# Retention and ELU layer on one core: the first block's retention in whole chunks of 128 tokens

## The chip, the cores and the metric

The kernel runs on one core of one Trainium2 chip. The metric is the device time of one execution in microseconds (us), the median of three runs. An engine [...] waits at an instruction until the semaphores that it names have come. The engines are called PE (TensorE, matrix products; its weight loads are listed apart as PEld), DVE (VectorE), ACT (ScalarE), POOL (GpSimd) and SP (SyncE, which here only issues DMAs).

## The reference

Retention with 8 heads of 64 over 4 sequences of 768 tokens, then a layer with an ELU between two weight matrices:

```
gamma[h] = 1 - 2**(-5 - h);  scale = 1/sqrt(64)
for t:  state = gamma * state + k[t] v[t]^T ;   y[t] = scale * q[t] state
x = y as (3072 tokens, 512)
h = x @ w_in            # 512 x 2048
g = h if h > 0 else exp(h) - 1
out = g @ w_out         # 2048 x 512
```

All of it is in 32-bit floats. The powers of gamma are taken out of the recursion: v is scaled by `gamma**-t / 8` (table `vf`), the result by `gamma**t` (table `etab`, seen as `powers`), and between the two the retention is a causal product without decay: the scores q k^T are masked to the past and multiplied with v, and q times the state (the sum of k v^T over all earlier pieces) is added.

## The kernel before, in words

The 3072 tokens go through in six blocks of 512. A block is four chunks of 128 tokens; one DMA brings a chunk (`load`, L110): q and k turned, with two heads above one another in the 128 partitions, and k and v with tokens in the partitions. The weights come in 16 pieces of 1 MB as 64-bit patterns (`load_piece`, L142) and are decoded into floats: two or three ACT steps (`prepare`, L164 to L168), then DVE steps (`decode`, L190 to L194). The step that takes the high words (`hi`) is ACT's L168, or DVE's L190 if `by_vector` is set. Pieces 0, 2, 4 and 6 are the halves `w_a` of the first matrix, pieces 1, 3, 5 and 7 the halves `w_b`.

The order of the work of each engine is written out by hand: instructions stand in each queue in the order in which the program calls for them. Generators (`decode` with `take`, `plain_first` as `inner`, `outputs_of_first`) are drawn on step by step to lay their parts between one another. Two things concern the change.

**Retention of a block (sub-chunks of 64 tokens).** Every product is a tile of 64 rows by 64 columns of the PE array, 64 elements long, so four of them can lie in the array at once. Per chunk there are 16 products of each of four kinds: scores (L307, from `score_products`), the sum k v^T of each half chunk (L338, `state_products`), scores times v (L394, `within`) and q times the state (L409, `across`). There is one state for every 64 tokens (`state`, `state_sum`, L348 or L350). The mask is a 64 by 64 triangle (`cmask`, L328 or L318). [...] the work is cut in two, and a small DVE copy (`seen`, L426 or L378) between the halves makes PE wait for the first half. DVE takes the result out of the PSUM times `powers` (L433 or L384) into `xb`.

In the first block chunk 0 and chunk 1 go one by one (`score_products`, `mask_pair`, `outputs_of_first`), chunks 2 and 3 as a pair (`scores(0, 1)`, `states(0, 1)`, `outputs(0, 1)`). The later blocks use the pair form throughout.

**First matrix on the first block (`plain_first`).** There are 16 tiles of 128 output rows over 512 tokens, four products each. Tiles 0 to 4 are done by halves of 256 tokens, because the second half of the tokens comes late: tile 0 in its first half even by chunks of 128 tokens. Tiles 5 to 15 are done in one go (L521). Tile k is in the PSUM bank "aabd"[k], tile 4 in a bank of the pool `ps_r` (`hp`). Tiles 0 to 3 need pieces 0 and 1, tile 4 needs piece 2. Behind every tile ACT and DVE form the ELU (L477, L478, L481).

At the start PE has nothing to do until the first chunk lands: one blank product of 512 columns and 28 blank products of 64 columns run (L1106, L1110). Three more blank products lie between the first steps (one of 256, two of 512 columns, `unread`).

The table `etab` for tokens 0 to 255 is built by ACT at the start (L249); the rest is built between the two halves of piece 0's `prepare` (argument `between`).

## Time and profile before

| | us |
|---|---|
| three runs | 633.62, 634.01, 636.01 (median 634.01) |
| the profiled execution, its own time | 632.87 |
| its span, first to last instruction | 630.9 |
| PE busy in the span | 624.8 (99%) |
| DVE, ACT, POOL busy | 483.1, 253.3, 21.8 |
| granted clock of TensorE | 1.00 |

The span is 1.97 us shorter than the execution's own time. A page of the profile and further views are used: sums by stretches of time; the timeline, which gives for each group of instructions its start, how long it lasts, engine, line, operation and tile, count, and in brackets how long the engine had been idle before it and what ended that; and the waits, which say who waited for whom. A product of 32-bit floats appears as two records of PE, so that "x8" on a line of PE is four products.

### The profile page before, as it was taken

How to read it: one execution, taken by the hardware profiler on the slowest of the kernel's cores; microseconds unless marked ns; L12 is line 12 of the kernel's file. 1: busy time of each engine (PE TensorE's matmuls, PEld its weight loads, DVE VectorE, ACT ScalarE, POOL GpSimd, SP SyncE). 2: the span in 40 equal slices, each digit the busy share in tenths (PEclk: the TensorE clock that was granted, in tenths of full speed). 3: DMA queues.
4: the chain of work that ended last, by engine and by line, in shares of the span. 5: the costliest groups of instructions: out<-in, count | busy, mean ns of one | idle time of the engine just before them, and what ended most of it. 6: DMA issues, size and time to landing. Idle time of an engine off the chain costs nothing.

```text
span 630.9 us, 16128 instructions
## 1 busy us (share of the span) xinstructions
PE 624.8 (99%) x6680; PEld 560.1 (89%) x6680; DVE 483.1 (77%) x884; ACT 253.3 (40%) x472; POOL 21.8 (3%) x25
## 2 busy tenths in 40 slices
PE   8999999999999999999999999999999999999998
PEld 5864578888899999889999989999988999988997
DVE  5779789989789675699685588777489877558975
ACT  6698635015541114653112646111465211366311
POOL 1021000000000000200000200000110000000000
PEclk9999999999999999999999999999999999999999
DMA  8698669689287888405888702888810798600794
GB/s 331 278 406 291 188 210 268 196 267 316 81 311 248 239 255 299 180 2 174 274 266 292 282 2 64 264 284 296 310 73 12 216 308 252 217 18 2 232 309 162
DMA packets 75897, 136.85 MB, mean 217 GB/s; under 512 B 6320, under 2 KB 31792, under 8 KB 70704
## 3 DMA queue, kind: packets, MB, share of 16 engines
q1 hardware_dynamic: 75824, 135.82, 64.8%
q8 instruction: 53, 0.87, 0.5%
q14 instruction: 20, 0.16, 0.1%
HBM read 114.56 MB, written 21.23 MB: 215 GB/s over the span
## 4 chain that ended last, share of the span: by engine, by line
PE 77%; SPq 1%; DVE 1%; DMA 1%; issue 0%; ACT 0%; ACTq 0%; DVEq 0%
PE pa L955 20%; PE pa L913 10%; PE pd L955 10%; PE pb L955 5%; PE pa L867 5%; PE pb L913 4%; PE pa L740 4%; PE qa L913 3%; PE pd L867 2%; PE qd L913 2%; PE pd L913 2%; PE pd L740 2%; PE y L394 1%; PE sc L307 1%; PE y L409 1%; PE kv L338 1%
## 5 line engine op out<-in xcount | busy, mean ns | idle before, releaser
L963 ACT COPY ms<-pa 128x128 f32<-128x128 f32 x104 | 27.7, 266 | 146.7 <-PE pa L955 146.7
L955 PE MATMUL pa<-ts,wq 128*128 128x128 f32 x560 | 74.2, 275 | 0.0
L955 PE MATMUL pd<-ts,wq 128*128 128x128 f32 x552 | 73.5, 276 | 0.0
L955 PEld LDWEIGHTS pa<-ts,wq 128*128 128x128 f32 x560 | 68.5, 192 | 0.4
L955 PEld LDWEIGHTS pd<-ts,wq 128*128 128x128 f32 x552 | 67.1, 192 | 0.6 <-DVE res L967 0.2
L955 PE MATMUL pa<-gC,wq 128*128 128x128 f32 x480 | 64.7, 278 | 0.0
L478 ACT ACTIVATE r<-r 128x512 f32<-128x512 f32 x96 | 60.5, 630 | 3.1
L955 PEld LDWEIGHTS pa<-gC,wq 128*128 128x128 f32 x480 | 59.0, 192 | 1.5 <-issue 0.3
L477 ACT ACTIVATE r<-gC 128x512 f32<-128x512 f32 x64 | 39.9, 624 | 32.4 <-DVE gC L921 32.4
L967 DVE TENSOR_TENSOR res<-pd,ms 128x128 f32<-128x128 f32 x68 | 19.5, 287 | 39.6 <-PE pd L955 38.4
L481 DVE SCALAR_TENSOR_TENSOR gC<-r,gC 128x512 f32<-128x512 f32 x64 | 44.0, 719 | 0.7 <-ACT r L478 0.7
L829 DVE TENSOR_TENSOR ts<-gC,ts 128x512 f32<-128x512 f32 x60 | 41.3, 688 | 1.0
L829 DVE TENSOR_TENSOR ts<-gC 128x512 f32<-128x512 f32 x60 | 41.0, 684 | 0.0
L281 POOL TENSOR_TENSOR chunk<-chunk,vf 128x512 f32<-128x512 f32 x16 | 20.0, 1251 | 428.8 <-DMA chunk<-in_qkv_dram 345.8
L955 PE MATMUL pb<-gC,wq 128*128 128x128 f32 x240 | 31.7, 275 | 0.0
L988 ACT COPY res<-pa 128x128 f32<-128x128 f32 x34 | 9.0, 266 | 55.0 <-PE pa L955 55.0
L955 PEld LDWEIGHTS pb<-gC,wq 128*128 128x128 f32 x240 | 29.2, 192 | 0.0
L690 ACT COPY m<-pa 128x512 f32<-128x512 f32 x24 | 13.9, 581 | 30.2 <-PE pa L740 16.3
L921 DVE TENSOR_TENSOR gC<-qa,gC 128x512 f32<-128x512 f32 x8 | 5.5, 692 | 25.0 <-PE qa L913 18.3
L913 PE MATMUL pa<-xt,w_b 128*128 128x256 f32 x96 | 23.0, 382 | 0.0
L913 PE MATMUL pa<-xt,w_s 128*128 128x256 f32 x96 | 23.0, 382 | 0.0
L913 PE MATMUL pa<-xb,w_a 128*128 128x256 f32 x96 | 22.7, 379 | 0.0
(255 smaller groups left out, 1244.3 us busy)
## 6 DMA issues: line engine op xcount, KB each, us to landing
wq<-scratch_dram SPq DMA_DIRECT2D x277, 256.0 KB, 4.3
chunk<-in_qkv_dram SPq DMA_DIRECT2D x23, 1024.0 KB, 8.6
wraw<-in_w_dram SPq DMA_DIRECT2D x15, 1024.0 KB, 6.0
out_dram<-res SPq DMA_DIRECT2D x14, 256.0 KB, 3.8
scratch_dram<-gT SPq DMA_DIRECT2D x12, 256.0 KB, 4.3
scratch_dram<-m SPq DMA_DIRECT2D x12, 192.0 KB, 6.0
scratch_dram<-so SPq DMA_DIRECT2D x4, 512.0 KB, 4.6
scratch_dram<-wi SPq DMA_DIRECT2D x2, 1024.0 KB, 6.4
```

Source lines behind the costliest of these rows:

```text
L281: eng.tensor_tensor(out=kv[:, 1], in0=kv[:, 1], in1=vf[:, i].unsqueeze(2).to_broadcast([C, H, D]), op=ALU.mult)
L477: nc.scalar.activation(e, h, AF.Relu, scale=-1.0)
L478: nc.scalar.activation(e, e, AF.Exp, scale=-1.0)
L481: nc.vector.scalar_tensor_tensor(g, e, -1.0, h, ALU.add, ALU.max)
L690: nc.scalar.copy(m, ps)
L740: nc.tensor.matmul(ps[:, fi, :], lhsT=w[:, fi, j2, :], rhs=x[:, j2, :], start=(begin and fi == 0 and j2 == 0), stop=(j2 == 1), skip_group_ ...
L829: sub = lambda o, x, y: nc.vector.tensor_tensor(out=o, in0=x, in1=y, op=ALU.subtract)
L867: nc.tensor.matmul(ps[:, f, :], lhsT=lhs[f], rhs=xs[j][k], start=(begin and f == 0), stop=True, skip_group_check=True,)
L913: nc.tensor.matmul(ps[:, fi, :], lhsT=w[:, fi, j2, :], rhs=x[:, j2, :], start=(j in (1, 7) and fi == 0 and j2 == 0), stop=(j2 == 1), skip_ ...
L955: nc.tensor.matmul(ps, lhsT=w[:, f, :], rhs=ts[j][k][:, f, :], start=(begin and f == 0), stop=(f == 3), skip_group_check=True,)
L963: nc.scalar.copy(m, ps)
L967: nc.vector.tensor_tensor(out=o, in0=x, in1=y, op=ALU.add)
```

## The change

For the first block alone, retention is done in chunks of 128 tokens (`whole_...`). Per chunk there are 8 products of each kind in place of 16:

- scores: 64 rows by 128 columns of the array, 128 long (all of the 128 by 128 scores of a head, also those that the mask sets to zero);
- scores times v: 128 rows by 64 columns, 128 long;
- q times the state: 64 by 64, 128 long, not for chunk 0;
- sum k v^T: 128 rows by 64 columns, 64 long.

There is one state per chunk and one addition per state. The mask is the 128 by 128 triangle `causal`; masked scores go partly over k in the chunk's buffer, partly to a new tile `pt`. The copies `seen` are gone. Chunks 2 and 3 are taken one by one, with tile 2 of the layer between their scores. Tile 4 is done in one go; tile 3 has its first half by chunks of 128 tokens. Blank products: 22 in place of 28 short ones; of the three `unread` one of 512 stays. The rest of `etab` is built after piece 1's `prepare`; the second half of piece 0 has its high words taken by DVE.

```diff
-        for k in range(5):
-            hp = bank("aabd"[k]) if k < 4 else ps_r.tile([P, 2, TH], FP32, name="hp", tag="r")
-            banks.append(hp.rearrange("p a b -> p (a b)"))
-            if k == 0:
-                part(0, slice(0, C))
+        for k in range(4):
+            banks.append(bank("aabd"[k]).rearrange("p a b -> p (a b)"))
+            if k in (0, 3):
+                part(k, slice(0, C))
                 yield
-                part(0, slice(C, 2 * C))
+                part(k, slice(C, 2 * C))
...
+    def whole_scores(m):
+        qk = raw[m][0]
+        sc = [ps_r.tile([P, HP, C], FP32, name="sc", tag="r") for _ in range(2)]
+        for p in range(HP):
+            for a in range(2):
+                nc.tensor.matmul(
+                    sc[a][:, p, :], lhsT=qk[rows(a), 1, p, :], rhs=qk[rows(a), 0, p, :],
+                    start=True, stop=True, skip_group_check=True,
+                )
+        more = hpool.tile([P, TB], FP32, name="pt", tag="h")
+        whole[m] = sc, (qk[:, 1], more.rearrange("p (h c) -> p h c", c=C))
+
+    def whole_mask(m, a):
+        sc, pt = whole[m]
+        nc.vector.tensor_tensor(
+            out=pt[a], in0=sc[a], in1=causal.unsqueeze(1).to_broadcast([P, HP, C]), op=ALU.mult
+        )
+
+    def whole_within(m, y, a):
+        pt, kv = whole[m][1], raw[m][1]
+        for u in range(2):
+            for c in range(2):
+                nc.tensor.matmul(
+                    y[a][rows(c), u, :], lhsT=kv[:, 1, head(a, u, c), :], rhs=pt[a][:, 2 * u + c, :],
+                    start=(u == 0), stop=(m == 0), skip_group_check=True,
+                )
+
+    def whole_across(m, y):
+        q = raw[m][0]
+        for u in range(2):
+            for c in range(2):
+                for a in range(2):
+                    p = 2 * u + c
+                    nc.tensor.matmul(
+                        y[a][rows(c), u, :], lhsT=state(0, 2 * m)[rows(a), p, :], rhs=q[rows(a), 0, p, :],
+                        start=False, stop=True, skip_group_check=True,
+                    )
+
+    def whole_products(m):
+        kv = raw[m][1]
+        t = ps_r.tile([P, HP, D], FP32, name="kv", tag="r")
+        for p in range(HP):
+            for a in range(2):
+                nc.tensor.matmul(
+                    t[rows(a), p, :], lhsT=kv[:, 0, 2 * p + a, :], rhs=kv[:, 1, 2 * p + a, :],
+                    start=True, stop=True, skip_group_check=True,
+                )
+        return t
+
+    def whole_sum(m, t):
+        if m:
+            nc.vector.tensor_tensor(out=state(0, 2 * m + 2), in0=t, in1=state(0, 2 * m), op=ALU.add)
+        else:
+            nc.vector.tensor_copy(state(0, 2), t)
+
+    def whole_end(m, y):
+        c = slice(m * C, (m + 1) * C)
+        for a in range(2):
+            j = slice(2 * a, 2 * a + 2)
+            nc.vector.tensor_tensor(out=xb[:, j, c], in0=y[a], in1=powers[:, j, c], op=ALU.mult)
+
+    def whole_place(m):
+        ts = [bank("bd"[a]) if m < 2 else ps_r.tile([P, 2, TH], FP32, name="y", tag="r") for a in range(2)]
+        return [t.rearrange("p a b -> p (a b)")[:, 0:TH].rearrange("p (u t) -> p u t", u=2) for t in ts]
```

The order of the first block's calls, written out by hand, after the change:

```
unread(1, TB); 22 short blank products
whole_scores(0); whole_mask(0, 0); scale_v(0); whole_mask(0, 1)
y = whole_place(0); whole_within(0, y, 0)
t = whole_products(0); whole_sum(0, t); whole_within(0, y, 1); whole_end(0, y)
unread(1, TB)
whole_scores(1)
prepare(2, by_vector=(False, True)); piece = decode(True); take(); take()
scale_v(1); whole_mask(1, 0); whole_mask(1, 1); take()
inner = plain_first(); next(inner)                    # tile 0, chunk 0
y = whole_place(1); whole_within(1, y, 0); whole_within(1, y, 1); whole_across(1, y)
whole_end(1, y); take()
t = whole_products(1); whole_sum(1, t); take()
prepare(2, by_vector=True); powers_of(slice(2 * C, S))
next(inner)                                           # tile 0 chunk 1, tile 1 first half
piece = decode(); take()
whole_scores(2); next(inner)                          # tile 2 first half
scale_v(2, True); whole_mask(2, 0); whole_mask(2, 1); take()
whole_scores(3); scale_v(3, True)
y = whole_place(2); whole_within(2, y, 0); whole_within(2, y, 1); whole_across(2, y)
t = whole_products(2); whole_mask(3, 0); whole_end(2, y); whole_mask(3, 1); whole_sum(2, t)
take(); prepare(2); next(inner)                       # tile 3, chunk 0
y = whole_place(3); whole_within(3, y, 0); whole_within(3, y, 1); whole_across(3, y)
next(inner); whole_end(3, y)                          # tile 3, chunk 1
piece = decode(True); take(); take()
t = whole_products(3); whole_sum(3, t)
take(); take(); take(); prepare()
```

After it come the second halves of tiles 0 to 3 and the tiles 4 to 15, as before.

## The prediction

> **What bounds the kernel now.** First the sums by stretches, cut where PE's work changes its nature: to 5.15 us (before the first chunk), to 15.92 (chunks 0 and 1), to 38.21 (chunks 2 and 3, tiles 0 to 4), then the rest.

> ```profile
> core 0: us, PE busy (x) PEld busy (x) DVE busy (x) ACT busy (x) POOL busy (x), PEclk, DMA share, GB/s
> 0.00:5.15 5.15, 3.70 (x58) 2.09 (x59) 2.40 (x23) 2.60 (x5) 1.56 (x8) 1.00 0.63 173
> 5.15:15.92 10.77, 9.56 (x258) 6.76 (x255) 6.83 (x19) 7.85 (x14) 0.17 (x1) 1.00 1.02 411
> 15.92:38.21 22.29, 21.96 (x337) 18.68 (x337) 17.03 (x32) 15.39 (x21) 0.46 (x1) 1.00 0.77 307
> 38.21:120.00 81.79, 81.79 (x731) 54.81 (x730) 71.21 (x109) 50.52 (x57) 5.86 (x4) 1.00 0.80 264
> ```

> The first column is the length, the second PE's busy time. From 38.21 PE never stops, and the waits of PE over the whole span are all of the first 28 us; the chain of waits is 77% PE. So whatever the change does must show as the time at which tile 5 (L521) starts, 38.21 before, and it goes one to one to the end. In the second stretch PE is covered by blank products and waits for DVE and DMA. Here is the third:

> ```profile
> 15.92 3.10 PE L497 MATMUL pa<-xb,w_a 128*128 128x128 f32 x16
> 18.93 1.99 PE L497 MATMUL pb<-xb,w_b 128*128 128x256 f32 x8
> 20.86 1.16 PE L307 MATMUL sc<-chunk 64*64 64x64 f32 x64
> 21.84 1.11 PE L338 MATMUL kv<-chunk 64*64 64x64 f32 x64
> 22.88 1.99 PE L497 MATMUL pd<-xb,w_b 128*128 128x256 f32 x8
> 24.81 1.50 PE L394 MATMUL y<-chunk 64*64 64x64 f32 x63
> ...
> 27.09 0.69 PE L409 MATMUL y<-chunk 64*64 64x64 f32 x32 [0.26 <-DVE seen L378]
> 27.78 1.97 PE L497 MATMUL hp<-xb,w_a 128*128 128x256 f32 x8
> ```

> The reader is to see that scores and sums take about 1 us each for two chunks, but L394 and L409 take 27.78 - 24.81 = 2.97 us: about 1.1 us of it are waits for states and for `seen`. That is what can be won, with 0.25 us of wait for piece 1 before 18.93.

> **Prices on PE.** A product is two records. An undisturbed four products of 128 columns take 0.89 us (190.12 to 191.01 below), of 256 columns 1.73 us (38.21 back to 36.49). The next lines are a group of the later blocks, and one of chunk 0:

> ```profile
> 186.11 1.06 PE L955 MATMUL pa<-ts,wq 128*128 128x128 f32 x8
> 187.10 2.10 PE L307 MATMUL sc<-chunk 64*64 64x64 f32 x128
> 189.12 1.16 PE L955 MATMUL pa<-gC,wq 128*128 128x128 f32 x8
> 190.12 1.06 PE L955 MATMUL pb<-gC,wq 128*128 128x128 f32 x8
> 191.01 1.06 PE L955 MATMUL pa<-gC,wq 128*128 128x128 f32 x8
> ```

> ```profile
> 8.42 0.45 PE L409 MATMUL pd<-chunk 64*64 64x64 f32 x8
> ```

> Small products go in steps: L409 at 14.68, 14.73 and 14.79 us starts four records each time, 0.058 us apart. 32 such steps are 1.87 us, L307 takes 2.02 to the next start, L955 before it 0.99 instead of 0.89 and after it 1.00: one excursion to small tiles and back costs 0.35 us beyond the work, 0.13 going in and 0.22 coming out. The one line of L409 is chunk 0's, where only one row half has a state: 8 records in 0.45 us, of which 0.22 is the length of the last. One after another at 0.058 they would need 0.63, so two column halves on the same rows do run side by side.

> [...] the modes 64x128 and 128x64 stand nowhere in the trace of before. [...] the blanks of 64 columns step at 0.107 us, L307 at 5.15 still does, and at 10.66 the step is 0.058.

> **The change on PE, per chunk.** Before: 16 products of a kind are 8 steps, 0.47 us, four kinds 1.87 us. After: scores, two side by side, 128 long: 8 products = 16 records = 8 steps of 0.112 (half of 0.89 by 4), 0.89 us. Scores times v: the same, 0.89. q times state: four side by side, 0.45. Sums: two side by side, 64 long, 0.47. Total 2.70, so 0.83 us more per chunk, because the scores that the mask kills are now computed and multiplied. More modes too: see below.

> **DVE.** 128x256 masks (L328) at 0.38 each become 128x512 at 0.60 to 0.69:

> ```profile
> 7.07 0.75 DVE L328 TENSOR_TENSOR chunk<-sc,cmask 128x256 f32<-128x256 f32 x2
> 22.07 1.29 DVE L318 TENSOR_TENSOR chunk<-sc,cmask 128x512 f32<-128x512 f32 x2 [0.35 <-PE sc L307]
> ```

> Against that fall six `seen` (0.16 to 0.25) and four additions of states (0.42). Per block DVE stays about equal; its order matters more.

> **Chunks 0 and 1, walked.** Landings, from issue and time to landing in the DMA view: chunk 0 at 5.1 (q, k) and 6.4 (k, v), first half of piece 0 at 8.1, chunk 1 at 10.6, second half of piece 0 at 12.6, piece 1 at 15.0, chunk 2 at 17.5, chunk 3 at 20.2. None of these is moved: SP's queue starts the same. The six blank products fewer end 0.3 us sooner (3 of their 14 steps of 0.107) and lie before 5.15, where PE waits for the landing: nothing, with that landing as cover; without it they would give 0.3. The two `unread` that go (0.70 and 0.9 us) lay in waits: nothing either. Scores of chunk 0 start at 5.15, half at the slow clock, ready about 6.65; mask 7.39, v scaled 7.99, PE goes on at 8.04 and is through by 9.4; results in `xb` at 10.3, where before it was 10.05. Piece 0's first half is decoded at 11.35 (11.44 before): equal. Chunk 1's scores start at 10.66, as before, bound by the landing, and end 0.42 later; masks ready at 12.56 and 13.16 (12.71 before). But then nothing waits for `seen`: scores times v to 13.66, q times state to 14.25, results in `xb` at 14.85 and 15.2 (before 15.85), and the sums end at 14.86. Tile 0's second chunk starts at **15.06 instead of 15.92**. Tile 1 needs piece 0's second half: its DVE step (L194) comes behind the results, done at 15.8; tile 1 starts at 16.05. High words by DVE (L190, 0.42) lie ahead of that, at 13.3, in DVE's wait for chunk 1's products.

> **From there to tile 5.** Work in order: tile 0 0.89, tile 1 1.73, scores 0.89, tile 2 1.73, scores 0.89, chunk 2's other products 0.89 + 0.45 + 0.47, tile 3 0.89, chunk 3's 0.89 + 0.45, tile 3 0.89, sums 0.47, second halves of four tiles 6.91, tile 4 in one go 3.45: 21.9 us. Before, the same stretch held 20.2; the difference is twice the 0.83 per chunk. Changes of mode: 4 from the layer into retention (0.13), 4 back (0.22), and 4 between forms of retention, not in the trace: bounds 0 and 0.22, I take 0.15, near the two measured. Sum 2.0 us against 0.7 before (two excursions). Tile 5 then starts at 15.06 + 21.9 + 2.0 = **38.95, 0.7 us later** than 38.21.

> Does something else come later still? Chunk 2 is there at 17.5, PE asks at 17.9; chunk 3 at 20.2, asked at 20.9. DVE by the same walk: mask of chunk 2 at 20.3, piece 1's second half 21.9, v of chunk 3 22.5, its first mask 23.1. PE's sums of chunk 2 need that one's bank (four in `ps_r`) at 23.5: 0.4 to spare. The second mask is done at 25.0, PE needs its bank at 25.2: 0.2 to spare. These two waits are new and thin: behind them in PE's queue stand tile 3 and all that follows, so a late mask goes through to the end. ACT's moved table (four of 0.64, at 17.9 to 20.5) sits in ACT's wait for piece 2 (landing 22.7) and is needed at 23.6. Tile 4 needs piece 2 decoded by 35.5: about 30. Its load, and that of pieces 3 to 5, wait for decodes that move by about -1 to +1.4 us; they were used 10 us after landing. Chunk 4's load stands behind piece 5's, unmoved.

> So 1.1 + 0.25 us of waits go and 0.86 is won before 15.06; 1.7 of work and 1.3 of drains come.

> **Rivals.** (1) *The forecast*, +0.7: 632.87 + 0.7 = 633.6 for the profiled execution. The median of the runs shown lies 1.1 above that execution, so 634.7 for the median. With drains at 0 or 0.22 inside retention it is +0.1 to +1.0.
> (2) *Drains hidden everywhere.* Then 15.06 + 21.9 = 37.0, -1.2: 632.8. For it: much of a drain can lie under waits. Against: the 0.35 us of the later blocks, where nothing waits.
> (3) *Slower: full-height column halves don't run side by side.* Shown is it only for 64 rows (L409). If 128x64 goes one after another, scores times v cost 0.89 and sums 0.47 more per chunk: chunks 2 and 3 2.7, chunk 1 1.36, chunk 0 about 0.6 (the rest hides behind chunk 1's landing): +4.7, 639.4. It is slower by over 0.5% from about half of that loss on.
> (4) *DVE's thin margins fail* (0.2 to 0.4 us), or the clock stays halved longer after fewer blanks (chunk 0's products at double price, 1 us, half behind chunk 1's landing): +0.8 more, 635.5.

> **Chances.** (1) 0.58, (2) 0.17, (3) 0.08, (4) 0.14; 0.03 for a larger gain that I can't place: all waits of the first 38 us are worth less than 3 us. A measurement of this kernel (runs 633.6 to 636.0) can tell 0.5%, 3.2 us, from no change. So faster 0.03, within 0.5% 0.88, slower 0.09. The range 632.4 to 637.4 takes in (1), (2), (4) and the scatter of the runs.

> **What would show it.** Tile 0's second chunk at about 15.1 and tile 5 at about 38.9; scores of a chunk in about 0.9 us; records of L422 (scores times v) in pairs 0.112 apart, else (3); gaps at each change of mode of 0.1 to 0.2, else (2); idle of PE before the sums of chunk 2 or chunk 3's first product, else not (4). Wrong it would be if PE after 39 us waited for weights.

## The result

| | before | after |
|---|---|---|
| runs side by side | 633.62, 634.01, 634.50, 636.01 | 640.52, 640.72, 641.17, 642.97 |
| median | 634.25 | 640.94 |
| ratio of the medians, 95% interval | | 1.0107, 1.0078 to 1.0137 |
| the profiled execution, its own time | 632.87 | 640.72 |
| its span | 630.9 | 638.7 |

The changed kernel is 6.7 us slower. The forecast of 634.7 and its range, up to 637.4, both miss. One of the rivals had named 639.4, and it too is wrong: its reason (column halves that don't run side by side) isn't in the trace, as the first fence shows.

**The first block is nearly as forecast.** The timeline of PE after the change, from tile 0's second chunk to tile 5 (start, length, engine, line, operation and tile, records, idle before and its cause):

```profile
15.27 2.97 PE L522 MATMUL pa<-xb,w_a 128*128 128x128 f32 x16
18.17 1.16 PE L405 MATMUL sc<-chunk 64*128 64x128 f32 x16
...
22.28 0.66 PE L422 MATMUL y<-chunk 128*64 128x128 f32 x8
22.77 0.61 PE L422 MATMUL y<-pt,chunk 128*64 128x128 f32 x8
23.30 0.67 PE L433 MATMUL y<-chunk 64*64 64x128 f32 x16
23.90 0.69 PE L443 MATMUL kv<-chunk 128*64 128x64 f32 x16
24.52 1.16 PE L522 MATMUL pd<-xb,w_b 128*128 128x128 f32 x8
...
35.94 4.46 PE L545 MATMUL pa<-xb,w_a 128*128 128x512 f32 x10
```

Tile 0's second chunk starts at 15.27 (forecast 15.06). Scores of a chunk take 1.10 us to the next start (19.27): 0.89 of work and 0.21 for the change of mode behind it. The 16 records of L422 take 23.30 - 22.28 = 1.02 us with a change of mode; one after another they would need 16 x 0.112 = 1.79. So 128x64 halves do run side by side. L433 takes 0.60, as forecast (0.45 + 0.15), and L443 0.62 (0.47 + 0.15). No line has a wait in brackets, so DVE's thin margins held. The five products in the last line start at 35.94; the first four are tile 4, which takes 3.44, and tile 5 starts at 39.38: forecast 38.95, before 38.21, so +1.17 instead of the forecast +0.7.

**The rest isn't.** The forecast ended there: tile 5's delay was to go one to one to the end. But the last product comes 7.5 us later than before. The sums by stretches of the changed kernel from tile 5 on (length, then busy time of PE, PEld, DVE, ACT, POOL; granted clock, DMA share, GB/s):

```profile
39.38:88.95 49.57, 49.57 (x581) 26.29 (x579) 39.86 (x61) 34.55 (x44) 4.79 (x4) 1.00 0.71 254
88.95:95.00 6.05, 4.19 (x12) 3.25 (x12) 5.77 (x10) 3.49 (x3) 0.00 (x0) 0.73 1.03 288
95.00:638.70 543.70, 538.06 (x5442) 504.50 (x5441) 410.69 (x741) 187.64 (x387) 12.93 (x12) 1.00 0.63 203
```

Up to 88.95 PE is busy without a break, as before. Then come six microseconds in which it is busy for 4.19 and the granted clock is 0.73, and 543.70 - 538.06 = 5.6 us without work are spread over the rest, of which about 3 were there before too (630.9 - 624.8 = 6.1 in all, 3.0 of it in the first three stretches that the prediction shows). The waits of PE (who waited for what; us in total, times, longest) of the changed kernel:

```profile
PE pd L635 <- DVE gC L506: 1.9, 1, 1.9
PE pb L422 <- issue: 1.5, 1, 1.5
PE pa L1130 <- DVE blank L207: 1.5, 1, 1.5
PE y L393 <- issue: 1.3, 1, 1.3
PE kv L322 <- issue: 0.9, 1, 0.9
```

L1130 stood in the kernel before as L1106, also 1.5. L422's 1.5 ends at 8.22, behind chunk 0's scores, where the prediction had PE wait for DVE until 8.04; so "issue" alone isn't yet a sign of anything, and this gap is no part of what follows. New, and past tile 5, are three: one wait for DVE and two for nothing that a semaphore shows ("issue"). Here they are on the changed kernel's timeline of PE:

```profile
88.09 1.03 PE L635 MATMUL x<-h,w_s 128*128 128x256 f32 x4
90.98 1.42 PE L635 MATMUL pd<-h,so 128*128 128x256 f32 x4 [1.86 <-DVE gC L506]
205.44 1.39 PE L322 MATMUL kv<-chunk 64*64 64x64 f32 x78
207.75 0.92 PE L322 MATMUL kv<-chunk 64*64 64x64 f32 x34 [0.92 <-issue]
325.56 0.57 PE L393 MATMUL y<-chunk 64*64 64x64 f32 x25
327.39 0.34 PE L393 MATMUL y<-chunk 64*64 64x64 f32 x7 [1.26 <-issue]
```

The same three places before:

```profile
87.79 1.03 PE L611 MATMUL pd<-h,so 128*128 128x256 f32 x4
200.93 2.08 PE L338 MATMUL kv<-chunk 64*64 64x64 f32 x112
319.58 0.65 PE L409 MATMUL y<-chunk 64*64 64x64 f32 x32
```

There the product into bank d (it is number 7 of the seven of `second_of_first`, X[7]) starts with no wait, and the 112 and the 32 records of the later blocks run through. Matching the two kernels' products one by one gives the account of the 7.5 us: +1.17 at tile 5, unchanged to 88 us; +2.0 at X[7]; +1.4 to 1.8 in the four microseconds behind it, where records of 256 columns start 0.43 us apart instead of 0.216; -0.4 in small gains; +1.1 at L322; +1.5 to 1.8 at L393.

### The profile page after: what moved, and what is told of

Read it like the earlier page. It is cut to its first block, busy times and chain, and to the rows that moved or that the text cites. A ratio compares the mean times of both kernels' runs of the same rounds, so it can differ in the third digit from the quotient of the medians.

```text
span 638.7 us, 15583 instructions
## 1 busy us (share of the span) xinstructions
PE 628.3 (98%) x6408; PEld 562.0 (88%) x6408; DVE 484.1 (76%) x880; ACT 252.6 (40%) x471; POOL 20.3 (3%) x25
## 4 chain that ended last, share of the span: by engine, by line
PE 97%; DVE 1%; issue 1%
PE pa L979 20%; PE pa L937 10%; PE pd L979 10%; PE pb L979 5%; PE pa L891 5%; PE pb L937 4%; PE pa L764 4%; PE pa L545 3%; PE qa L937 3%; PE x L635 3%; PE pa L635 2%; PE pd L891 2%; PE qd L937 2%; PE pd L937 2%; PE pd L764 2%; PE y L378 2%
## 5 line engine op out<-in xcount | busy, mean ns | idle before, releaser
L987 ACT COPY ms<-pa 128x128 f32<-128x128 f32 x104 | 27.7, 266 | 149.4 <-PE pa L979 149.4
L979 PE MATMUL pa<-ts,wq 128*128 128x128 f32 x560 | 74.2, 275 | 0.0
L979 PE MATMUL pd<-ts,wq 128*128 128x128 f32 x552 | 73.5, 276 | 0.0
L979 PEld LDWEIGHTS pa<-ts,wq 128*128 128x128 f32 x560 | 68.5, 192 | 0.4
L979 PEld LDWEIGHTS pd<-ts,wq 128*128 128x128 f32 x552 | 67.1, 192 | 0.6 <-DVE res L991 0.2
L979 PE MATMUL pa<-gC,wq 128*128 128x128 f32 x480 | 64.6, 278 | 0.0
L979 PEld LDWEIGHTS pa<-gC,wq 128*128 128x128 f32 x480 | 59.0, 192 | 1.4 <-issue 0.2
L280 POOL TENSOR_TENSOR chunk<-chunk,vf 128x512 f32<-128x512 f32 x16 | 18.5, 1157 | 438.1 <-DMA chunk<-in_qkv_dram 415.3
L979 PE MATMUL pb<-gC,wq 128*128 128x128 f32 x240 | 31.7, 275 | 0.2 <-issue 0.2
L979 PEld LDWEIGHTS pb<-gC,wq 128*128 128x128 f32 x240 | 29.3, 192 | 0.3 <-issue 0.3
L714 ACT COPY m<-pa 128x512 f32<-128x512 f32 x24 | 13.9, 581 | 31.4 <-PE pa L937 14.3
L937 PE MATMUL pa<-xb,w_a 128*128 128x256 f32 x96 | 22.7, 379 | 0.0
```

Of the source, the lines that this page charges most:

```text
L937: nc.tensor.matmul(ps[:, fi, :], lhsT=w[:, fi, j2, :], rhs=x[:, j2, :], start=(j in (1, 7) and fi == 0 and j2 == 0), stop=(j2 == 1), skip_ ...
L979: nc.tensor.matmul(ps, lhsT=w[:, f, :], rhs=ts[j][k][:, f, :], start=(begin and f == 0), stop=(f == 3), skip_group_check=True,)
L987: nc.scalar.copy(m, ps)
```

## The theories

**Bank.** `plain_first` now does tiles 4 to 15 in the banks "aabd"[k % 4], twelve tiles; before it was tiles 5 to 15, eleven. So the last tile lies in bank d, where before it lay in bank b. X[7] is the first product of the next step that wants one of those banks, it is in d, and it must wait until DVE has read the last ELU out of d. What stands behind it in PE's queue came no sooner: PE was idle for 1.86 us. DVE's last ELU, after and before:

```profile
90.24 0.68 DVE L506 SCALAR_TENSOR_TENSOR gC<-r,pd 128x512 f32<-128x512 f32 x1
```

```profile
89.10 0.67 DVE L481 SCALAR_TENSOR_TENSOR gC<-r,pb 128x512 f32<-128x512 f32 x1
```

It ends at 90.92, and PE goes on at 90.98. Before, it ended at 89.77, two microseconds after X[7] had begun, and harmed nobody, for it was in b.

**Clock.** Behind the pause the granted clock (1.00 is full speed) is at half: 0.50 from 91.68 to 95.09 us, which is the 0.73 above.

**Fetch.** By this theory PE has run out of instructions at the two "issue" gaps. The page of the changed kernel lists a queue named for them (packets, MB, share):

```profile
q8 instruction: 51, 0.84, 0.5%
```

Before there were 53. Each of the 51 is 16,384 bytes long. The page counts 6408 products' records and 6408 weight loads on PE after, 6680 and 6680 before: 251 and 252 instructions for each packet. With the 254 semaphore steps and drains of PE that the trace after lists besides, it is 13,070 instructions in 51 packets, 256 for each. A 32-bit product is two records and two loads, so 64 products use up a packet. Large products take a long time for 64 (256 columns at 0.43 us: 28 us), small ones 32 steps of 0.058 us = 1.9 us. The DMA view of 205.0 to 206.4, the stretch ahead of the first gap, has one packet:

```profile
q8 instruction: 1, 0.02, 4.1%
```

It begins at 205.3, and PE goes on at 207.75, 2.4 us later; at the second gap the packet begins at 325.0, PE goes on at 327.39, again 2.4 us. When these packets began, PE had 1.5 and 1.1 us of work in hand (to 206.83 and 326.13). The change takes out 136 products net (6 blanks, 2 `unread`, 64 in chunks 0 and 1, 64 in chunks 2 and 3). That is two packets and **8 products**: every border between packets behind the first block is moved by 8 products, and with it the place in the code where PE may run dry. At 47 of the 50 borders in the changed kernel's trace PE goes on without a gap; by this theory it stands still where a border falls into 64x64 products.

**Rival: blanks.** The six blanks fewer (or other work ahead of 15 us) leave PE or its clock in a worse state, and the count of instructions has nothing to do with it.

In the expectations, quoted as they were on record before each run, A is the bank together with the clock, C the fetch and D the blanks; B is what else could be, and differs from run to run. Ratios are against the kernel before on the same chip.

## The experiments

**Both causes one by one.** First the banks of X[7] and X[3] exchanged in the changed kernel, so that X[7] lies in b, which has been read early:

```diff
-        X |= {j: bank(x) for j, x in ((7, "d"), (6, "a"), (5, "a"), (3, "b"))}
+        X |= {j: bank(x) for j, x in ((7, "b"), (6, "a"), (5, "a"), (3, "d"))}
```

> The changed kernel with one edit: in the first block's second product, the banks of X[7] and X[3] are exchanged (X[7] in bank b, X[3] in bank d). Theory A (handover of a bank): the change moved the last tile of the layer from bank b to bank d, so X[7] has to wait for the last ELU, 2.0 us, and the idle TensorE then runs 1.8 us longer at half clock. Then this kernel takes 3.8 us less than the changed kernel: about 637.1 us, and the wait of X[7] is gone. Rival B (the loss comes from the first block's dearer retention and what it displaces, whatever the bank): the wait turns up elsewhere and the time stays at 640.9, within 0.7.

Measured 639.77 (before: 634.37), ratio 1.0089 [1.006, 1.0119]. The wait at X[7] is gone, and the clock is full. But the waits of PE (the profile is of the slowest of the five runs, 643.01) are now:

```profile
PE y L393 <- issue: 2.1, 1, 2.1
PE pb L979 <- issue: 0.9, 1, 0.9
PE kv L322 <- issue: 0.6, 1, 0.6
PE pa L764 <- DVE m L619: 0.5, 1, 0.5
```

The exchange makes a new wait (L764): DVE's sums out of the banks, which give L764 its banks a and b, begin only when the product into b is through, at 137.18, where in the changed kernel they began at 134.47. The "issue" gaps grow to 3.6 us. The expectation of some 637 missed. That PE, coming earlier to a border, gains nothing if the fetch is what it waits for is a likely reason, but not shown by this run.

Then the count alone: eight blank products of 64 columns behind the scores of chunk 0, where PE waits for DVE anyway.

```diff
     whole_scores(0)
+    for n in range(8):
+        nc.tensor.matmul(
+            warm[rows(n % 2), 0:D], lhsT=blank[rows(0), 0:D], rhs=blank[rows(0), 0:D],
+            start=True, stop=True, skip_group_check=True,
+        )
     whole_mask(0, 0)
```

> The changed kernel with eight blank products of 64 columns more, where TensorE waits for the first mask. Theory C (instruction fetch): two stalls of 1.1 and 1.5 us inside the small products of blocks 2 and 3 (sums at 206 us, q times state at 326 us) come because TensorE's instructions arrive in pieces of 16 KB and a border of a piece now falls inside these dense stretches; the change took 136 products away, which is 8 short of a multiple of 64, and 64 products fill a piece. Eight more put the borders back where they were: both stalls gone, 2.4 us less, about 638.5 us. Rival B: eight covered products change nothing, 640.9.

Measured 638.92 (before: 634.37), ratio 1.0059 [1.0037, 1.008]. The gaps near 206 and 326 us are gone with eight products that run 200 us earlier, in a wait; X[7] waits 1.9 as it did, and one gap of 1.1 stands at another L393 (303.8 us).

Both edits together:

> Both edits together. Theories A and C add up: 3.8 + 2.4 us less than the changed kernel, 634.7 us, which is what the first block alone costs (+1.2 by the trace, tile 5 at 39.4 instead of 38.2) against the kernel before, 634.2 to 635.5. Rival B: 640.9. If only one of A and C holds: 637.1 or 638.5.

Measured 636.98 (before: 634.37), ratio 1.0043 [1.0027, 1.0059]: better than either, not as good as hoped. The profile has L764's new wait (0.8 with its neighbour), 0.9 for a DMA of weights (`wq`) and 0.3 at L393. The exchange isn't a clean cure of the bank.

**The count alone, in the kernel before.** If eight products are what matters, taking eight of the 28 covered blanks from the old kernel must harm it, with nothing else changed:

```diff
-    for n in range(28):
+    for n in range(20):
```

> The kernel before with 20 instead of 28 short blank products and nothing else. They end before the first chunk lands, so the eight that go are worth 0 by themselves. Theory C: the borders of the instruction pieces now fall where they fall in the changed kernel, and the same two stalls appear in the small products of blocks 2 and 3: slower by 2 to 2.5 us, 636.5. Rival B: 634.2, within 0.5.

Measured 642.29 (before: 634.37), ratio 1.012 [1.0062, 1.0178]: 7.9 us lost (in four runs from 637.6 to 644.6) by leaving out eight products that do nothing, more than the fetch theory had asked for. The waits of PE show why, and the timeline has the gap within one product of where the changed kernel has it (80 of 112 records done, there 78):

```profile
PE y L394 <- issue: 1.8, 1, 1.8
PE kv L338 <- issue: 1.2, 2, 0.6
PE y L409 <- issue: 1.2, 1, 1.2
```

```profile
205.82 1.40 PE L338 MATMUL kv<-chunk 64*64 64x64 f32 x80
207.85 0.91 PE L338 MATMUL kv<-chunk 64*64 64x64 f32 x32 [0.64 <-issue]
```

L394's 1.8 lies in the first block, at 27.70; there too the clock fell (0.70 from 27.7 to 33.3), and tile 5 came at 41.94 instead of 38.21. The blank rival explains a loss as well, so the next run tells them apart: 20 blanks at the start as here, and eight behind chunk 0's scores. The start is as poor in blanks as in the last run, the count is restored.

```diff
-    for n in range(28):
+    for n in range(20):
...
     score_products(sc, 0, 0, 0)
+    for n in range(8):
+        nc.tensor.matmul(
+            warm[rows(n % 2), 0:D], lhsT=blank[rows(0), 0:D], rhs=blank[rows(0), 0:D],
```

> The kernel before with 20 short blank products at the start and the missing eight put behind the first scores, in TensorE's wait for the first mask. Theory C (the count up to each point decides): back to 634.4, within 0.7. Rival D (fewer blanks leave TensorE's clock or start worse, which is why 20 were slow): it stays at 640 or more.

Measured 634.89 (before: 633.51), ratio 1.0015 [0.999, 1.004]: no difference from before that is clear of the noise, and no "issue" gap among PE's longer waits. The blank rival falls: it asked for 640 or more. What counts is the number of instructions ahead, not what they do at the start.

**The bank alone, in the kernel before.** Only the loops of `plain_first` are taken from the change (tiles 0 to 3 by halves, 4 to 15 in one go). The number of products is that of before.

```diff
-        for k in range(5):
-            hp = bank("aabd"[k]) if k < 4 else ps_r.tile([P, 2, TH], FP32, name="hp", tag="r")
+        for k in range(4):
...
-        for k, (n, w, row, fi) in enumerate(tiles[5:]):
+        for k, (n, w, row, fi) in enumerate(tiles[4:]):
             hp = bank("aabd"[k % 4]).rearrange("p a b -> p (a b)")
```

> The kernel before with the changed kernel's tiles (0 to 3 by halves, tile 3's first half by chunks, tile 4 in one go in bank a) and the old retention: the same number of products, so the borders of the instruction pieces stay. Theory A (handover of a bank): the last tile comes to lie in bank d, X[7] waits 2.0 us for its ELU; 636.4, and up to 638.2 where the pause lowers TensorE's clock. Rival B (the dearer retention is the cause): 634.4, within 0.5.

Measured 637.83 (before: 633.51), ratio 1.0074 [1.0055, 1.0092], in the range expected. The wait is there without any of the new retention:

```profile
PE pd L610 <- DVE gC L481: 1.9, 1, 1.9
```

But the 4.3 us aren't the bank's alone. The same profile has two "issue" gaps in the first block, and the kernel before had none there:

```profile
24.81 1.08 PE L394 MATMUL y<-chunk 64*64 64x64 f32 x57 [0.76 <-issue]
28.54 0.49 PE L497 MATMUL pd<-xb,w_b 128*128 128x128 f32 x2 [0.30 <-issue]
```

Tile 5 starts at 39.23 instead of 38.21: 1.0 us is lost before any bank is handed over. The count ahead of L394 is that of before; but tile 3's first part ahead of it is half as long (128 columns instead of 256), and that PE is through with its work sooner after the packet began is a likely reason, not shown by this run. So some 3.3 us are left for the bank and the clock.

Does the pause bring down the clock? Two filler products of 512 columns into a spare bank, put ahead of X[7], keep PE busy while it waits; two blanks fewer at the start keep the count:

```diff
             for j in order:
+                if n == 0 and j == 7:
+                    fill = ps_r.tile([P, 2, TH], FP32, name="fill", tag="r").rearrange("p a b -> p (a b)")
+                    for _ in range(2):
+                        nc.tensor.matmul(
+                            fill, lhsT=w_a[0][:, 0, 0, 0, :], rhs=w_a_[:, 1].rearrange("p a b c d -> p (a b c d)")[:, 0:TB],
+                            start=True, stop=True, skip_group_check=True,
+                        )
```

> The kernel before with the changed tiles (last tile in bank d), with two products of 512 columns whose result nobody reads put ahead of X[7], and two short blanks fewer at the start so that the count stays from there on. The products (1.7 us) fit into the pause of 2.0 us. If the pause lowers TensorE's clock (the lower clock cost about 1.8 us in the profiles of the changed kernel and of the one with the tiles alone, not in the one with eight blanks), the clock stays up and only the wait is left: 633.5 + 2.0 + 0.3 = 635.8, and no 256-column product steps at 0.43 us. If the clock has nothing to do with the pause: as with the tiles alone, 637.8.

Measured 636.17 (before: 633.13), ratio 1.0046 [1.0031, 1.0061]. PE's timeline around X[7], without and with the filler:

```profile
90.83 1.13 PE L610 MATMUL pd<-h,so 128*128 128x256 f32 x4 [1.87 <-DVE gC L481]
91.80 1.70 PE L610 MATMUL pa<-h,so 128*128 128x256 f32 x4
```

```profile
90.12 1.88 PE L612 MATMUL fill<-w_a 128*128 128x512 f32 x4
92.16 1.13 PE L617 MATMUL pd<-h,so 128*128 128x256 f32 x4 [0.15 <-DVE gC L481]
93.12 1.03 PE L617 MATMUL pa<-h,so 128*128 128x256 f32 x4
```

The second pair of products, two of 256 columns into pa, takes 1.50 us to the next start (93.30) after the pause, and 0.87 (93.99) after the filler. The count isn't quite the same up to X[7], where this kernel is two products short; its profile, of the slowest of the five runs, has fetch gaps of 0.70 and 1.09 us ahead of there. So the steps behind the pause are the evidence on the clock, more than the difference of the times.

The mean clocks of the runs point the same way. With the pause at X[7] (the changed kernel, the one with eight blanks, the bank alone), 19 of 29 runs had a mean clock of 0.997 or less. Without it (this run, and the next two kernels with another bank) none of 21 had. Such a clock isn't proof of this pause, though: other kernels have it in some runs (3 of 90 of the kernel before; 3 of 4 with 20 blanks, where a fetch gap takes 1.8 us). The size is less firm: the runs of the kernel with eight blanks are at 636.6 and 637.7 with full clock and at 638.9 to 639.6 without, about 2 us, but for the bank alone the medians are 637.4 at full clock (7 runs) and 637.9 at 0.997 (9 runs), and four more runs at 0.995 took 639.2 to 642.5. Of the three profiles that have this pause, the clock fell behind 1.86 us in the changed kernel and behind 1.87 with the bank alone (a mean of 0.75 from 89 to 95 us); with eight blanks it stayed at 1.00 behind 1.86.

What sets the third apart isn't shown. In the changed kernel the pause ends at 90.98 and the clock falls at 91.68, for 3.41 us. The other kernels' waits of over 1.7 us go both ways: behind the 1.77 with 20 blanks, and the 2.40 and 2.39 of the last two kernels below, the clock fell; in the profiles with the banks exchanged (2.1) and with another bank and no blanks (1.8) the mean clock is 1.00. So the length of the pause alone doesn't decide it. No run was made to find out what does.

**Both cures, without the exchange.** Tile 4 goes back to a bank of `ps_r`, so that eleven tiles walk through "aabd" again, and the eight covered blanks are in:

```diff
-            hp = bank("aabd"[k % 4]).rearrange("p a b -> p (a b)")
+            hp = bank("aabd"[(k - 1) % 4]) if k else ps_r.tile([P, 2, TH], FP32, name="hp", tag="r")
+            hp = hp.rearrange("p a b -> p (a b)")
```

> The changed kernel with eight covered blank products and with tile 4 in a bank of ps_r, as before the change, so that the last tile lies in bank b again. Theories A and C: no wait of X[7], no stalls by fetch beyond those of the kernel before; what is left is the first block's own cost, +0.8 to +1.2 us against 634.4: 635.2 to 635.6. Rival: the change costs more in later blocks than a border and a bank (the time stays above 637).

Measured 634.45 (before: 633.51), ratio 1.0008 [0.9985, 1.003]. Its waits of PE are only these, both within the first 10 us, and X[7] has no wait:

```profile
PE pa L1131 <- DVE blank L207: 1.5, 1, 1.5
PE pb L422 <- issue: 0.9, 1, 0.9
```

```profile
39.74 1.45 PE L546 MATMUL pa<-xb,w_a 128*128 128x512 f32 x3
...
89.32 1.03 PE L636 MATMUL pd<-h,so 128*128 128x256 f32 x4
```

So the whole change, less these two side effects, costs 0.9 us by the medians, near what the forecast had said of the first block (+0.7); but the interval reaches from -1.0 to +1.9 us, and in this profile tile 5 starts at 39.74, 1.5 us late. Of the 6.7 us measured, some 5.8 belong to the two side effects.

The same without the eight blanks, to see the bank's share:

> The changed kernel with tile 4 in a bank of ps_r (last tile in bank b) and without the eight blanks. Theory A with C: X[7] doesn't wait, but both stalls by fetch in blocks 2 and 3 are there: 634.5 (both edits) + 2.4 = 636.9. If theory C were wrong: 634.5.

Measured 641.26 (before: 633.13), ratio 1.0122 [1.0096, 1.0148]. The expectation of 636.9 missed by far. With the pause cured PE waits longer at the borders (the profile is of the slowest of four runs):

```profile
PE y L393 <- issue: 4.3, 3, 1.8
```

The three gaps at L393 end at 79.2, 327.6 and 408.9 us. The first lies ahead of X[7], so the cured pause can't have made it. In the changed kernel the packet for the same border began at 74.26, PE crossed it at 77.67, 3.4 us later, without a gap. Why this kernel has one isn't shown.

So the bank's and the fetch's costs don't add up: the bank alone cured gains nothing (+8.1 against +6.7), the count alone cured gains 2.1 (+4.6), both gain 5.8. Eight idle products are worth 8.1 - 0.9 = 7.2 us here, as they were worth 7.9 - 1.4 = 6.5 in the kernel before; by the intervals of the ratios the first is certain to some 2 us, the second to some 4.

**A version from the parts that pay.** Whole chunks only for chunks 0 and 1, where waits went (tile 0's second chunk was 0.65 us earlier in the trace); chunks 2 and 3 and the tiles as before, and the eight blanks, so that exactly 64 products, one packet, fewer run than before:

```diff
-    whole_scores(2)
-    next(inner)
     scale_v(2, True)
-    whole_mask(2, 0)
-    whole_mask(2, 1)
-    take()
-    whole_scores(3)
     scale_v(3, True)
...
+    scores(0, 1)
+    states(0, 1)
```

> Whole chunks for chunks 0 and 1 only; chunks 2 and 3 and all tiles as before; the count of products differs from before by exactly 64, one instruction piece. If the first two chunks gain what the trace of the changed kernel shows (tile 0's second chunk at 15.27 instead of 15.92) and the later two lose it, this is 0.65 us faster than before: 633.7. If theory C is wrong about the count, stalls as in the changed kernel: 636 or more.

Measured 633.28 (before: 633.51), ratio 0.9986 [0.9971, 1.0]. Its median is 0.2 us below that of before, the only one of these kernels that isn't above it, but no gain is clear of the noise. Its timeline has one fetch gap left, in the first block, and tile 5 at 37.81, 0.4 earlier than before:

```profile
26.63 1.10 PE L522 MATMUL hp<-xb,w_a 128*128 128x256 f32 x4
28.32 1.02 PE L522 MATMUL hp<-xb,w_a 128*128 128x256 f32 x4 [0.58 <-issue]
...
37.81 2.74 PE L546 MATMUL pa<-xb,w_a 128*128 128x512 f32 x6
```

Can that gap be moved too? The same kernel with 16 covered blanks, and with 24:

> The version with whole chunks for chunks 0 and 1 only, with sixteen instead of eight covered blank products, so that every later border of an instruction piece lies eight products earlier in the work. Theory C: the time moves by microseconds with a count of covered products, either way (a border leaves the fetch stall of 0.7 us at tile 4's first half and may fall into another dense stretch): outside 632.6 to 634.0. Rival: eight covered products are worth nothing here, 633.3 within 0.7.

> The same with twenty-four covered blank products, borders sixteen products earlier. Theory C as for sixteen, another value; if this or the one with sixteen is free of the stall at tile 4 and of others, 632.5, the fastest of all. Rival: 633.3 within 0.7.

Measured 636.38, ratio 1.0053 [1.0035, 1.0071], and 637.92, ratio 1.0061 [1.0044, 1.0078] (before: 633.64). Both are worse; the hope for less than 633 missed. The border moves back into the 64x64 products of the first block, with 16 blanks first and with 24 second:

```profile
21.48 1.11 PE L322 MATMUL kv<-chunk 64*64 64x64 f32 x61
24.99 0.47 PE L322 MATMUL kv<-chunk 64*64 64x64 f32 x3 [2.40 <-issue]
```

```profile
21.81 0.87 PE L322 MATMUL kv<-chunk 64*64 64x64 f32 x45
25.07 0.90 PE L322 MATMUL kv<-chunk 64*64 64x64 f32 x19 [2.39 <-issue]
```

The gap moves by 16 records, that is eight products, for eight blanks. (With 16 blanks the profile, of the slowest of eight runs, has another gap of 1.5 us at 226.7.) The kernel with 8 blanks fits too: its border is due at record 61 + 16 = 77 from the start of L322, where the trace has no gap, and the next one 128 records (64 products) on, at 205; its gap at `hp` comes after 64 (L322) + 8 (`pd`) + 64 + 64 (L378, L393) + 4 = 204. That is the fetch theory to the product: the border stays with the count of instructions, not with the work. In both profiles the clock is 0.50 from 24.9 to 31.4 behind the gap.

The changed kernel's own trace bears it out when PE's instructions (weight loads, products, semaphore steps and drains) are counted from 0 in the order of their starts. Past the first block it has three "issue" gaps of over 0.15 us: 0.92 at 207.75, 0.17 at 306.63 (L979) and 1.26 at 327.39. All three lie at the same place in a packet: the number of the instruction behind the gap leaves 193, 193 and 194 when divided by 256. The gap at L422 doesn't (128). The trace also shows which borders cost nothing. From the start of a packet to PE's instruction with remainder 193 it is 2.44, 2.35 and 2.41 us at the three gaps, and 3.24 or more at the other 47 borders; in the kernel before it is 2.47 or more at all 52, and no border there has such a gap. The first gap is what the work in hand (1.52 to 206.83) lacks of 2.44, and the last what it lacks (1.15 to 326.13) of 2.41.

## Why the prediction was wrong

**The step that failed** is the one taken from the first table: "From 38.21 PE never stops", and so "whatever the change does must show as the time at which tile 5 (L521) starts, 38.21 before, and it goes one to one to the end." That PE never stopped was a fact of the kernel before; it was used as a property that the changed kernel would keep. Two things that the change altered without delay to tile 5 broke it later:

- *The bank of the last tile.* The prediction walked the banks up to tile 4 and looked for late weights after 39 us, not at who takes the banks of `plain_first` over. The diff shows `enumerate(tiles[4:])`. Tile 15 is (15 - 4) % 4 = 3, bank d; before it was (15 - 5) % 4 = 2, bank b; and X[7] of the next step is in d. Put into the kernel before, the new tiles cost 4.3 us: 1.0 of it by fetch gaps ahead of tile 5, and some 3.3 by the wait of 1.9 for the bank and the half clock behind it.
- *The six blank products.* "Nothing, with that landing as cover" is right for their time and wrong for their count. The prediction asked what work each edit adds or takes away, and left out that PE's instructions come in packets (16,384 bytes, 64 products in these traces), whose borders all move. With six blanks, two `unread` and 128 products gone, they move by eight. That was the larger and less stable cost: 6.5 and 7.2 us for eight products in two kernels without the other cause, but 2.1 in the changed kernel itself, where the other cause stays.

**What held.** Tile 0's second chunk within 0.21 us; the stretch from there to tile 5 24.11 us (forecast 23.9); work per kind; the changes of mode inside retention, the prediction's "drains", near 0.15 (0.13, 0.15 and 0.20); column halves side by side; DVE's margins. The net cost of the change as designed was forecast as +0.7 and is +0.9 by the kernel with both cures, though the runs can't tell that from nothing or from twice as much, and tile 5 was 1.2 us late in the changed kernel's profile. Rival (3) named a time near the measured one for a reason that the trace refutes: a number that fits isn't a mechanism. The prediction's slow clock at the start stays its estimate: the doubled steps of 0.107 us are measured, but the trace of before has no record of the clock ahead of 6.01 us.

**What stays open.** What makes a packet begin when it does: the changed kernel's trace gives the 2.35 to 2.44 us from there to PE at its three gaps, not the moment at which the packet is asked for. Which pauses bring down the clock, and why. How much the fall of the clock costs: at full clock the bank alone still loses 637.4 - 633.5 = 3.9 us; its wait is 1.9 and its fetch gaps, if they are as in the one profile, 1.0, so about 1 us has no cause. A count for the changed kernel better than eight more wasn't looked for.

## What to carry to other kernels

Where one engine is busy to the end, an edit near the start has two more outputs than its delay: how many instructions come ahead of later code, and which buffers the next stage inherits; look at both before calling a delay "one to one". An ablation that changes the count of small products must put idle ones back in a covered place, to the same count modulo a packet (here 64 products), or it measures the fetch. And when a stage's number of tiles changes, follow the rotation to its last tile and to the first product of the next stage that wants that bank.
